# Pacing the input loads of a fused attention and token-mixing kernel by waiting on the landing of earlier loads

## The chip, the cores and the metric

The kernel runs on one core of one Trainium2 chip. The metric is the device time of one execution in microseconds (us). A run counts as slow when it is over 1.5% above the fastest run of the same kernel. Spans quoted from a profile are one or two us shorter than the times, as they run from the first to the last instruction.

## The reference

Chunked attention over 8 batches, 8 heads, 576 positions and head size 64, in chunks of 64 positions, then a token mixer over the 512 channels. Cut to what matters:

```python
scores = scale * np.matmul(q_c, k_c.transpose(0, 1, 2, 4, 3))   # chunks of 64 x 64
attn = softmax(scores)
x = np.matmul(attn, v_c)                       # -> [8, 576, 512]
wq, wk = x @ w_q, x @ w_k                      # 64 columns each
W_tok = scale * np.einsum('bsd,btd->bst', wq, wk)
mixed = np.einsum('bst,btd->bsd', W_tok, x)
out = np.maximum(mixed, 0.0) @ w_out           # [8, 576, 512], float32
```

The inputs q, k and v are 9.4 MB each in float32; the output is 9.4 MB.

## The kernel before

GpSimd (POOL) issues all loads; they cast float32 to float16 on the way. A batch takes twelve of them in this order: four large pieces of q and k, four half as large, two small and two large pieces of v. They go to fixed buffers (one q and k buffer per batch, four v buffers for eight batches). The load of the output weights follows batch 1. The code is cut; `...` stands for what is left out.

```python
TR = ((0, 6), (6, NT))                 # NT = 9: q and k in a part of 6 and one of 3
VP = ((0, 12, 0), (12, NP, 1))         # NP = 36: v in a part of 12 and one of 24

def load_qk(b, part):
    a, e = TR[part]
    for src, dst in ((q, qn), (k, kn)):
        for u in range(2):
            nc.gpsimd.dma_start(dst[b][CH*u : CH*u+CH, a:e, :], ...)

def load_v(b):
    for a, e, w in VP:
        for u in range(2):
            h = CH * (u ^ w)
            nc.gpsimd.dma_start(vt[b % VB][h : h+CH, a:e, D*u : D*u+D], ...)

def load(b):
    load_qk(b, 0)
    load_qk(b, 1)
    load_v(b)
    if b == 1:
        nc.gpsimd.dma_start(wout[:], ...)

load(0)
# ... identity, four small loads of the query and key weights ...
for b in range(1, VB):                 # VB = 4
    load(b)
# load(b + 4) is put after the attention of batch b in the plan of units
# ... a written plan orders transposes (T), scores (S), attention (A) and the
#     matmuls of the mixer (X Q K G M O) of several batches on TensorE;
#     all stores are held back until the v buffer of batch 7 is being filled ...
```

A piece of q or k from the larger part carries the weight 1 in what follows; a piece of v from the larger part carries 1.33. I call the loads of one batch q1 q2 k1 k2 q3 q4 k3 k4 v1 v2 v3 v4.

The softmax here doesn't subtract the row's maximum and nothing guards it: scores larger than these inputs give would overflow.

## Time and profile before

| | before |
|---|---|
| time, median of 4 runs | 127.09 us (126.0 to 128.57) |
| span of the profiled run (fast) | 124.5 us |
| TensorE busy | 100.3 us, 81% |
| first q piece of batches 3 to 7 lands at | 41.7, 52.7, 62.9, 73.6, 83.7 us: 10.5 us per batch |
| last load lands at | 93.1 us |
| k transposes of batches 3 to 7 start at | 48.0, 59.3, 71.8, 82.9, 94.7 us: 11.7 us per batch |

The landings come from the trace's semaphore events; each load has sixteen (one per DMA engine, by the section on semaphores that the prediction cites), and the sixteenth is its landing. The k transposes show the pace that TensorE keeps when nothing starves it. The loads run 1.2 us per batch faster than that. The lines of the profile are in the prediction below; here is the view of GpSimd's waits (engine, line, what it waited for; us in total, times, longest):

```profile
POOL kn L107 <- DMA vt<-in_v_dram: 7.6, 11, 1.5
POOL vt L118 <- issue: 2.4, 5, 0.8
POOL kn L107 <- DMA wout<-in_moe_w_out_dram: 1.5, 1, 1.5
```

GpSimd waits little, and mostly when eight loads are outstanding, the most that its eight semaphores in rotation allow.

### The profile page before, as it was taken

The page shows a single profiled execution, that of the slowest core. Times are in us where ns is not written, and L with a number is a line of the kernel's source. Part 1 is how long each engine was busy: PE and PEld are TensorE (multiplying, and loading weights), DVE is VectorE, ACT ScalarE, POOL GpSimd, SP SyncE. Part 2 cuts the span into 40 slices and gives each one's busy share as a digit, 9 for nine tenths or more (in the row PEclk, how much of TensorE's full clock was granted, in tenths as well). Part 3 has the DMA queues.
Part 4 walks back from the last instruction along what each step waited for, and adds up shares of the span by engine and source line. Part 5 has one row for each costly group of instructions (what it writes and reads, how often), then busy time and mean ns, then how long its engine had stood idle before and what let it go on. Part 6 is the DMA issues. An engine that isn't in the chain of part 4 may idle for free.

```text
span 124.5 us, 4600 instructions
## 1 busy us (share of the span) xinstructions
PE 100.3 (81%) x1959; PEld 61.8 (50%) x1959; DVE 75.4 (61%) x138; ACT 80.9 (65%) x138; POOL 72.0 (58%) x107
## 2 busy tenths in 40 slices
PE   6803280799639999999997899999999995999970
PEld 2203150587426565645764457656674674544420
DVE  5529079746873689759938695798599557400000
ACT  7992320514636486695687598686878793688960
POOL 6999799954769779589669958966400000000000
PEclk9997555559996899999999999999999999999998
DMA  1999999999999999999999999999999989964494
GB/s 10 171 183 156 155 167 169 153 152 196 194 156 165 189 175 143 186 189 150 159 182 167 152 188 185 145 189 189 154 223 342 383 325 380 381 238 170 169 348 160
DMA packets 63129, 24.55 MB, mean 197 GB/s; under 512 B 39556, under 2 KB 58500, under 8 KB 63108
## 3 DMA queue, kind: packets, MB, share of 16 engines
q0 software_dynamic: 57936, 14.82, 129.0%
q1 hardware_dynamic: 5172, 9.44, 20.3%
q8 instruction: 15, 0.25, 0.8%
q14 instruction: 6, 0.05, 0.1%
HBM read 29.62 MB, written 9.44 MB: 314 GB/s over the span
## 4 chain that ended last, share of the span: by engine, by line
PE 47%; DMA 17%; POOL 13%; DVE 11%; ACT 5%; issue 5%; DVEq 0%; ACTq 0%; POOLq 0%
PE banks L341 20%; DMA vt<-in_v_dram 9%; DMA kn<-in_k_dram 8%; PE banks L208 6%; DVE kT L181 6%; PE banks L273 5%; PE banks L234 5%; POOL kn L107 5%; PE banks L258 4%; POOL qn L107 4%; POOL vt L118 4%; DVE xn L244 3%; PE banks L306 3%; PE banks L320 2%; DVE rec L243 1%
## 5 line engine op out<-in xcount | busy, mean ns | idle before, releaser
L341 PE MATMUL banks<-wout,rmx 128*128 128x512 f16 x144 | 36.5, 386 | 0.0
L118 POOL DMA_DIRECT2D vt<-in_v_dram x32 | 27.3, 859 | 6.2 <-issue 2.4
L216 ACT ACTIVATE est<-banks 128x768 f16<-128x768 f32 x24 | 18.6, 810 | 17.8 <-PE banks L208 17.7
L244 DVE TENSOR_TENSOR xn<-banks,rec 128x640 f16<-128x640 f32 x32 | 26.4, 824 | 1.1
L107 POOL DMA_DIRECT2D kn<-in_k_dram x32 | 20.9, 668 | 9.1 <-DMA vt<-in_v_dram 7.6
L208 PE MATMUL banks<-qT,kT 32*64 32x64 f16 x1152 | 13.8, 218 | 11.5 <-DVE qT L181 5.3
L181 DVE STREAM_TRANSPOSE kT<-kn 128x768 f32<-128x768 f32 (+1 forms) x16 | 19.3, 1205 | 4.9 <-DMA kn<-in_k_dram 4.9
L328 ACT ACTIVATE rmx<-banks 128x576 f16<-128x576 f32 x32 | 19.6, 660 | 3.8 <-PE banks L320 3.7
L107 POOL DMA_DIRECT2D qn<-in_q_dram x32 | 21.1, 681 | 0.9 <-POOLq L417 0.8
L208 PEld LDWEIGHTS <-kT 32*64 32x64 f16 x1152 | 11.9, 112 | 14.8 <-DVE kT L181 10.0
L341 PEld LDWEIGHTS <-rmx 128*128 128x128 f16 x144 | 12.3, 98 | 13.6 <-issue 2.2
L234 PE MATMUL banks<-vt,est 128*64 128x130 f16 x288 | 15.8, 241 | 3.4 <-DMA vt<-in_v_dram 1.8
L243 DVE RECIPROCAL rec<-banks 128x10 f32<-128x10 f32 x32 | 6.8, 213 | 17.3 <-PE banks L234 14.2
L263 DVE COPY xt<-banks 128x576 f32<-128x576 f32 x16 | 11.9, 754 | 7.3 <-PE banks L258 5.2
L234 PEld LDWEIGHTS <-est 128*64 128x64 f16 x288 | 11.5, 119 | 8.0 <-issue 3.7
L258 PE MATMUL banks<-identw,xn 128*128 128x128 f32 x80 | 13.3, 307 | 2.2 <-DVE xn L244 1.6
L258 PEld LDWEIGHTS banks<-identw,xn 128*128 128x128 f32 x80 | 10.4, 156 | 5.6 <-DVE xn L244 2.6
L181 DVE STREAM_TRANSPOSE qT<-qn 128x768 f32<-128x768 f32 (+1 forms) x16 | 12.1, 757 | 0.5 <-DMA qn<-in_q_dram 0.5
L359 ACT COPY qn<-banks 128x512 f32<-128x512 f32 x16 | 9.5, 595 | 4.0 <-DVE xt L263 2.4
L359 ACT COPY kn<-banks 128x512 f32<-128x512 f32 (+1 forms) x15 | 9.2, 626 | 3.4 <-PE banks L341 3.1
L273 PE MATMUL banks<-xt,wqk 128*128 128x288 f16 x64 | 9.5, 289 | 0.0
L282 ACT CAST wT<-banks 128x576 f16<-128x576 f32 x8 | 5.1, 640 | 5.2 <-PE banks L273 5.2
(36 smaller groups left out, 88.4 us busy)
## 6 DMA issues: line engine op xcount, KB each, us to landing
out_dram<-qn SPq DMA_DIRECT2D x16, 256.0 KB, 3.9
out_dram<-kn SPq DMA_DIRECT2D x14, 256.0 KB, 2.9
qn<-in_q_dram POOLq DMA_DIRECT2D x16, 192.0 KB, 6.0
kn<-in_k_dram POOLq DMA_DIRECT2D x16, 192.0 KB, 6.8
vt<-in_v_dram POOLq DMA_DIRECT2D x16, 192.0 KB, 6.0
qn<-in_q_dram POOLq DMA_DIRECT2D x16, 96.0 KB, 6.9
kn<-in_k_dram POOLq DMA_DIRECT2D x16, 96.0 KB, 5.9
vt<-in_v_dram POOLq DMA_DIRECT2D x16, 96.0 KB, 5.2
```

The source lines that it names most:

```text
L107: nc.gpsimd.dma_start(dst[b][CH * u : CH * u + CH, a:e, :], src[b] .rearrange("h s d -> (h s) d") .rearrange("(u t p r) d -> u p t (r d)", ...
L118: nc.gpsimd.dma_start(vt[b % VB][h : h + CH, a:e, D * u : D * u + D], v[b] .rearrange("h s d -> (h s) d") .rearrange("(u g p) d -> u p g d ...
L181: nc.vector.transpose(out=o, in_=src[b].bitcast(F32)[:, a:e, :].rearrange("p t (r d) -> p t r d", d=32),)
L208: nc.tensor.matmul(a[h : h + CH, i, o : o + CH], lhsT=k_of(*x), rhs=q_of(*x), start=(e == 0), stop=(e == 1),)
L216: nc.scalar.activation(est[b % 2][s + n].rearrange("p i t c -> p i (t c)"), a[:, :, 0 : 2 * TS * CH], AF.Exp, scale=scale_attn,)
L234: nc.tensor.matmul(af[CH * (c % 2) : CH * (c % 2) + CH, o : o + W], lhsT=lhsT, rhs=rhs, start=True, stop=True,)
L244: nc.vector.tensor_tensor(out=xn[b % 2] .rearrange("p j (a u b d) -> p j a u b d", a=2, u=2, b=2)[:, :, h // 2, :, h % 2, :], in0=xv[:, :, ...
L258: nc.tensor.transpose(tx[:, j * P : j * P + P], xn[b % 2].bitcast(F32)[:, j, n * P : n * P + P], identw[:],)
L273: nc.tensor.matmul(a[:, h, 0:HS], lhsT=wqk[:, i, :], rhs=xt[b % 2][i // 2] .bitcast(F16) .rearrange("p (s e) -> p s e", e=2)[:, h * HS : h ...
L328: nc.scalar.activation(rmx[(b // 2) % 2].rearrange("p (h i) n -> p i h n", h=2)[:, i, :, o : o + HS], a[:, :, 0:HS], AF.Relu, scale=scale_moe,
L341: nc.tensor.matmul(a[:, x, :], lhsT=rmx[pr % 2][:, i, tl * P : tl * P + P], rhs=wout[:, 2 * (i % 2) + i // 2, :], start=(i == 0), stop=(i ...
L359: nc.scalar.copy(os_, a[:, 0:w, :])
```

## The change

Its intent is to keep only about four pieces outstanding, so that the pieces land in order and soon after their issue. Each load is given an estimate of its transfer time as a weight; it waits for the latest earlier load before which the weights still in flight sum to over 3.6. The diff is cut; `<semaphore wait>` stands for the object that describes the dependency.

```diff
+    AHEAD = 3.6
+    queue = []
+
+    def fetch(dst, src, us):
+        ins = nc.gpsimd.dma_start(dst, src).ins
+        ahead = 0.0
+        for name, u in reversed(queue):
+            if ahead + u > AHEAD:
+                tc.add_manual_dep(ins, name, <semaphore wait>, reason="pace")
+                break
+            ahead += u
+        queue.append((ins.name, us))
+
     def load_qk(b, part):
...
-                nc.gpsimd.dma_start(
+                fetch(
                     dst[b][CH * u : CH * u + CH, a:e, :],
...
+                    (e - a) / 6,
                 )
     def load_v(b):
...
-                nc.gpsimd.dma_start(
+                fetch(
...
+                    (e - a) / 18,
                 )
...
-            nc.gpsimd.dma_start(wout[:], ...)
+            fetch(wout[:], ..., 2.6)
```

More of the change, by code (lines that the diff above doesn't have):

```diff
@@ L101 @@
     of = out.rearrange("b s m -> (b s) m")
+    queue = []
[4 more added lines that the diff above has]
+            if ahead + u > AHEAD:
+                tc.add_manual_dep(
+                    ins,
+                    name,
+                    mybir.DependencyInfo(mybir.DependencyClass.Sync, mybir.DependencyReason.DATA),
+                    reason="pace",
+                )
+                break
+            ahead += u
+        queue.append((ins.name, us))
     def load_qk(b, part):
@@ L146, in load @@
         if b == 1:
-            nc.gpsimd.dma_start(wout[:], moe_w_out.rearrange("(i p) m -> p i m", p=P))
+            fetch(wout[:], moe_w_out.rearrange("(i p) m -> p i m", p=P), 2.6)
     nc.vector.memset(zero[:], 0.0)
```

## The prediction

> **What bounds the kernel now.** I read the page first: its busy shares, its forty slices and the list of DMA queues.
>
> ```profile
> span 124.5 us, 4600 instructions
> PE 100.3 (81%) x1959; PEld 61.8 (50%) x1959; DVE 75.4 (61%) x138; ACT 80.9 (65%) x138; POOL 72.0 (58%) x107
> ...
> PE   6803280799639999999997899999999995999970
> ...
> PEclk9997555559996899999999999999999999999998
> DMA  1999999999999999999999999999999989964494
> ...
> q8 instruction: 15, 0.25, 0.8%
> ...
> HBM read 29.62 MB, written 9.44 MB: 314 GB/s over the span
> ```
>
> One slice is 3.1 us. TensorE (PE) is broken up in the first twelve slices and close to full in all that follow. The DMA engines are full from the second slice until the loads end near 93 us. So there are two regimes: to about 37 us TensorE waits for data, from there to the end it has work all the time. The table of windows says the same with sums:
>
> ```profile
> 0.00:12.00 12.00, 5.47 (x110) 2.63 (x110) 6.77 (x30) 8.92 (x13) 10.87 (x21) 0.95 1.25 129
> 12.00:24.00 12.00, 5.47 (x205) 3.91 (x189) 7.09 (x12) 3.27 (x5) 11.33 (x18) 0.50 1.78 161
> 24.00:37.00 13.00, 9.17 (x180) 6.87 (x180) 8.85 (x15) 5.76 (x11) 7.98 (x13) 0.85 1.72 174
> 37.00:55.00 18.00, 17.67 (x398) 11.10 (x394) 12.39 (x20) 12.37 (x21) 14.48 (x22) 0.91 1.84 174
> 55.00:75.00 20.00, 18.53 (x409) 11.35 (x403) 15.97 (x25) 14.66 (x27) 16.34 (x24) 1.00 1.86 167
> ```
>
> The columns are the window, its length, busy time of PE, PEld, DVE, ACT and POOL, the granted clock, the DMA share and GB/s. TensorE is busy 20.1 of the first 37 us, and 36.2 of the next 38.
>
> Next came the chain of waits, for what ends the idle time. These are three places of it, all before 37 us:
>
> ```profile
> 7.92 6.29 DMA vt<-in_v_dram
> 14.20 0.28 issue
> 14.49 0.66 POOL kn L107
> ...
> 24.60 10.43 DMA kn<-in_k_dram
> 35.05 1.53 DVE kT L181
> 36.63 0.98 PE banks L208 x96
> ```
>
> The piece of k for batch 2 is issued at 24.60 and lands at 35.03; the transpose starts 0.02 us later, and the scores of batch 2 (S02) at 36.63. TensorE idles 2.15 us before them. That is the last wait for a load which I find: in the list of waits the 4.9 us of the k transposes on loads all lie before 37 us, and between 37 and 95 us no compute engine waits for a load. **The load stream matters only as far as it moves that landing at 35.0 us.**
>
> The first two lines above also show a limit that exists already. GpSimd (POOL) issues at 14.49, 0.29 us after a v piece issued eight transfers earlier landed. In the trace's semaphore numbers the loads rotate over eight semaphores, and each waits for the one eight before it. So at most eight are outstanding now; the change makes that about four.
>
> **What the Trainium skill says.** "DMA: Bandwidth & Descriptors", section "Anatomy of one DMA", puts the fixed cost of a GpSimd DMA at about 2.0 us and says that semaphore waits sit on the issuing sequencer, not on the DMA engines. The trace: the first piece is issued at 1.25, its descriptors take 0.78, and it lands at 4.61, so 2.58 us after them. With a transfer near 1.05 us that leaves 1.5 us fixed plus the issue: roughly agreed. The same page, "Specifications", gives about 358 GB/s of HBM per core. Here 29.62 MB are read from about 2.7 to 92.5 us, 330 GB/s, 92% of it: agreed, the stream is near its ceiling. The section "Why a DMA increments its semaphore by 16 and not by 1" says that sixteen engines each add one and only the sixteenth means landed. The trace has sixteen events per load. For the first piece they span 0.43 us, for the k piece that lands at 35.02 they span 2.86 us (first 32.16, median 33.11). "TensorE: Matmul & The Clock Gate", Part 1, says that the clock is halved after an idle window. Here it was 0.50 in 12 to 24 us, and the clock records also have 0.5 from 38.1 to 41.5 us, just after the stall: agreed.
>
> **The change part by part.** It removes and moves no transfer, no byte and no arithmetic. It adds a wait to each load except the first few and the four small loads of the query and key weights.
>
> *How deep the queue stays.* The weights in the diff are 1 four times, 0.5 four times, 0.67 twice and 1.33 twice: 10 per batch, and 2.6 for the output weights. First issues of later batches stand at 46.27, 56.78, 67.45 and 77.93 in GpSimd's timeline, 10.55 us per batch or 1.055 us per unit of weight. Walking the rule over a batch, the weight in flight with the new piece is between 3.33 (second q piece, second v piece) and 4.67, against eight pieces or about 6.7 today.
>
> *Whether that keeps the engines fed.* The round trip of a paced piece of weight 1 is 0.29 (landing to issue, above) + 0.68 (mean of the q and k issues, page rows 668 and 681 ns) + 2.58 (descriptors ready to landed) = 3.55 us. A depth of 4 covers 4.2 us, so 0.7 us is spare; the tightest, 3.33, covers 3.51 us, so 0.04 us is missing, once per batch. After the output weights only the two q pieces remain ahead of the next k piece, so 3 units or 3.17 us: 0.39 us missing, once. Up to the landing at 35 us the sum is some 0.5 us lost.
>
> *Start.* The v pieces of batch 0 now wait for k landings at 7.21, 8.61 and 9.64. The fourth is issued at about 10.5 instead of 8.89; the identity (about 0.5 us) and four unpaced weight loads of 0.6 us follow it on GpSimd, so the first q piece of batch 1 goes out at about 14.4 instead of 12.70. With 0.7 + 2.2 to 2.6 us it lands near 17.5 instead of 16.56. But the following pieces then land one unit apart, near 20.65 instead of 20.27: 0.4 us lost.
>
> *Spread.* The engines that run ahead are now held back. When one engine falls behind, the others can be no more than about 0.7 us ahead of it before they run dry, so the spread of 2.86 us should shrink to about 1. If the common limit is HBM, the late engine gets what the others leave, and the landing moves from 35.0 towards its median of 33.1: 1.0 to 1.9 us gained. If each engine is its own limit, the others merely idle. Then each stall of one engine stalls all. Such stalls exist: the fifteen instruction packets take 0.8% of sixteen engines' span, 0.008 x 16 x 124.5 / 15 = 1.06 us each, and three start before 35 us. That would cost 1 to 2 us.
>
> *Sum at that landing.* +0.5 +0.4 and then between -1.9 and +2, weighing a gain somewhat higher because that landing's spread is so large: -0.3 us, give or take 1.5. Behind it everything moves along, as TensorE is saturated.
>
> **The rivals.**
> 1. *A clear gain.* The landing comes 2 us earlier, so the gap of 2.15 us closes, and the half-clock window from 38.1 to 41.5 us, which costs up to 1.7 us, goes with it. For it: the gap lies just before the window. Against it: it needs nearly all of the spread and no bubble. About 124 us.
> 2. *A starved stream.* The waits let the load rate fall by a tenth, so that batch 3 is late too. Its k piece lands at 44.52 and is transposed at 48.04, 3.5 us of margin; batch 4's lands at 55.35 for 59.25, 3.9 us. The margins speak against it; the thin spare depth speaks for it. 129 to 131 us.
> 3. *Hidden anyway.* Loads take 10.55 us per batch and TensorE about 12 us, so from 37 us on the waits cost nothing, and v pieces already wait for their buffer. The loads may even end 2 to 4 us later; the held stores start at 89.8 us and have a reserve behind them in a tail bound by TensorE. Within 1% of before.
>
> **How range and chances follow.** Rival 3 with a shift of -0.3 us is the centre. The three times before are 126.0, 127.83 and 128.57 and the profiled run took 126.24, so 127.5 is a fair level for before and I put the changed kernel at 127.2. The shift of 1.5 us either way and the spread of the runs of 1.3 us give 124.6 to 129.8. Two per cent are 2.6 us: a gain of that size needs rival 1 in full, a loss needs rival 2. A pacing with weights as fine as these looks swept for, which tips the tails towards faster: 0.20, 0.65 and 0.15.
>
> **What would show it.** In the changed trace: no more than about four load pieces outstanding; GpSimd idle before nearly every load with a load as the releaser; median time to landing of q and k pieces down from 6 to 7 us to about 4; spread of the sixteen increments near 1 us. The k piece for batch 2 landing at 33.5 to 36 us decides the sign. TensorE's slices after 37 us should be as full as before. The prediction is wrong if the landing stays and the time moves (then the clock or the stores did it), or if a transpose after 40 us waits for a load (then the stream was starved).

## The result

The changed kernel takes **144.07 us** (median of four runs, 142.15 to 147.01) against 127.09. The ratio of the fast runs is 1.127, with a 95% interval of 1.103 to 1.150. Here and below a ratio is the mean time of one kernel's fast runs over that of the other's of the same rounds, so not quite the ratio of the medians. The prediction of 127.2, at most 129.8, was wrong, and the change is slower beyond doubt.

The profile after is of a run in the slow state (144.74 us; two of the four runs were fast, 142.15 and 143.4). Its main readings, the wait of q2 and what it costs, were found again in a profile of a fast run with that wait alone, below; its exact times hold for this run only. The page of the changed kernel, its busy shares, slices (3.6 us each here) and the first DMA queue:

```profile
span 143.0 us, 4618 instructions
...
PE   6604342889549977967876899698679996999920
...
PEclk9995555556986999999996899999999999999997
DMA  2999999999999599969994999999999999999994
...
q0 software_dynamic: 57936, 14.82, 109.7%
```

TensorE is no longer full from 37 us on: its row has 5s, 6s and 7s up to the loads' end at 116 us. The DMA row has dents (5, 6, 4). The same packets took about the same time in sum (109.7% of 143.0 us against 129.0% of 124.5 us) but overlapped less. GpSimd's waits in the changed kernel, where all loads are now issued from one line:

```profile
POOL qn L107 <- DMA vt<-in_v_dram: 20.2, 6, 4.5
POOL vt L107 <- DMA kn<-in_k_dram: 5.2, 7, 1.1
POOL qn L107 <- DMA qn<-in_q_dram: 2.4, 2, 1.3
```

A q piece waits for a v piece, six times, 20.2 us in all. The timeline of GpSimd shows where it stands in a batch (start, length, what, idle time before and what ended it):

```profile
67.78 3.48 POOL L107 DMA_DIRECT2D vt<-in_v_dram  x4 [1.29 <-PE banks L340]
71.53 0.66 POOL L107 DMA_DIRECT2D qn<-in_q_dram  x1 [0.28 <-issue]
76.05 0.66 POOL L107 DMA_DIRECT2D qn<-in_q_dram  x1 [3.86 <-DMA vt<-in_v_dram]
76.70 1.32 POOL L107 DMA_DIRECT2D kn<-in_k_dram  x2
```

It is q2: the weights of q1, v4 and v3 make 3.67, just over the limit, so it waits for v3 with only 2.33 units left in flight. The chain that ended last runs through the same place:

```profile
69.36 6.17 DMA vt<-in_v_dram
75.52 0.02 issue
75.55 0.02 POOLq L107
75.56 0.49 issue
76.05 0.43 POOL qn L107
```

v3 is issued at 69.36 and lands at 75.52, and q2 leaves at 76.05. The first pieces of batches 3 to 7 land at 48.4, 63.1, 77.2, 92.1 and 105.0 us: **14.1 us per batch instead of 10.5**, slower than the 11.7 us at which TensorE works. The transposes now wait for loads in the middle of the kernel (timeline of the changed kernel on VectorE, called DVE, which does them; the first k transposes of batches 3, 4 and 6):

```profile
54.02 1.57 DVE L201 STREAM_TRANSPOSE kT<-kn 128x768 f32<-128x768 f32 x1 [0.18 <-DMA kn<-in_k_dram]
68.35 1.58 DVE L201 STREAM_TRANSPOSE kT<-kn 128x768 f32<-128x768 f32 x1 [0.37 <-DMA kn<-in_k_dram]
...
96.63 1.66 DVE L201 STREAM_TRANSPOSE kT<-kn 128x768 f32<-128x768 f32 x1 [0.67 <-DMA kn<-in_k_dram]
```

These waits are short, 0.2 to 0.7 us. TensorE itself waits longer, for v pieces: 6.7 us in four waits between 40 and 112 us, where the kernel before had no wait of TensorE for a load between 37 and 95 us. There is one in each of batches 3 to 6, and it ends when v4, the last load of the batch, lands (the whole view of TensorE's waits in the kernel before from 37 to 95 us, then of the changed kernel from 40 to 112 us its first line, and the line of its timeline for batch 4, whose v4 lands at 76.20):

```profile
PE banks L306 <- issue: 1.0, 2, 0.6
PE banks L258 <- DVE xn L244: 0.4, 1, 0.4
PE banks L208 <- DVE kT L181: 0.2, 1, 0.2
...
PE banks L254 <- DMA vt<-in_v_dram: 6.7, 4, 2.2
...
76.25 0.54 PE L254 MATMUL banks<-vt,est 128*64 128x130 f16 x6 [2.04 <-DMA vt<-in_v_dram]
```

The span grew by 18.5 us (by 15.9 and 17.1 in the two fast runs, which have no profile). The k transpose of batch 7 starts 16.0 us later (110.70 against 94.74). From the scores after it to the last ACT copy both kernels take the same, 24.3 and 24.4 us. The remaining 2.4 us are at the end: from the end of that copy the last stores take 5.65 us instead of 3.2. The held stores were released at 112.95 us, not at 89.84, and were still in arrears when TensorE finished.

### The profile page after: what moved, and what is told of

Its sections match the earlier page's. It is cut to its first block, busy times and chain, and to the rows that moved or that the text cites. A ratio compares the mean times of both kernels' runs of the same rounds, so it can differ in the third digit from the quotient of the medians.

```text
span 143.0 us, 4618 instructions
## 1 busy us (share of the span) xinstructions
PE 104.5 (73%) x1959; PEld 64.2 (45%) x1959; DVE 75.8 (53%) x138; ACT 81.6 (57%) x138; POOL 72.0 (50%) x107
## 3 DMA queue, kind: packets, MB, share of 16 engines
q0 software_dynamic: 57936, 14.82, 109.7%
## 4 chain that ended last, share of the span: by engine, by line
DMA 47%; PE 19%; POOL 16%; issue 8%; DVE 4%; ACT 2%; POOLq 0%; DVEq 0%; ACTq 0%
DMA vt<-in_v_dram 21%; DMA kn<-in_k_dram 18%; POOL vt L107 10%; PE banks L361 9%; DMA wout<-in_moe_w_out_dram 5%; DMA qn<-in_q_dram 3%; POOL qn L107 2%; PE banks L254 2%; PE banks L326 2%; DVE xn L264 2%; POOL kn L107 2%; PE banks L340 2%; POOL wraw L176 2%; PE banks L228 2%; PE banks L293 2%
## 5 line engine op out<-in xcount | busy, mean ns | idle before, releaser
L361 PE MATMUL banks<-wout,rmx 128*128 128x512 f16 x144 | 37.5, 394 | 0.1
L107 POOL DMA_DIRECT2D qn<-in_q_dram x32 | 20.7, 655 | 24.8 <-DMA vt<-in_v_dram 20.2
L254 PE MATMUL banks<-vt,est 128*64 128x130 f16 x288 | 17.0, 246 | 10.7 <-DMA vt<-in_v_dram 9.6
L228 PE MATMUL banks<-qT,kT 32*64 32x64 f16 x1152 | 14.0, 219 | 14.5 <-DVE qT L201 5.9
L228 PEld LDWEIGHTS <-kT 32*64 32x64 f16 x1152 | 12.1, 114 | 18.1 <-DVE kT L201 12.7
L254 PEld LDWEIGHTS <-est 128*64 128x64 f16 x288 | 12.1, 121 | 16.4 <-issue 8.3
L361 PEld LDWEIGHTS <-rmx 128*128 128x128 f16 x144 | 12.6, 100 | 13.9 <-issue 2.6
L278 PEld LDWEIGHTS banks<-identw,xn 128*128 128x128 f32 x80 | 10.8, 161 | 6.3 <-DVE xn L264 3.1
L293 PE MATMUL banks<-xt,wqk 128*128 128x288 f16 x64 | 10.4, 308 | 0.0
L340 PE MATMUL banks<-wT,g 64*128 64x288 f16 x32 | 7.5, 287 | 2.6 <-DVE xn L264 1.8
```

The source lines that it names most:

```text
L107: ins = nc.gpsimd.dma_start(dst, src).ins
L228: nc.tensor.matmul(a[h : h + CH, i, o : o + CH], lhsT=k_of(*x), rhs=q_of(*x), start=(e == 0), stop=(e == 1),)
L254: nc.tensor.matmul(af[CH * (c % 2) : CH * (c % 2) + CH, o : o + W], lhsT=lhsT, rhs=rhs, start=True, stop=True,)
L278: nc.tensor.transpose(tx[:, j * P : j * P + P], xn[b % 2].bitcast(F32)[:, j, n * P : n * P + P], identw[:],)
L293: nc.tensor.matmul(a[:, h, 0:HS], lhsT=wqk[:, i, :], rhs=xt[b % 2][i // 2] .bitcast(F16) .rearrange("p (s e) -> p s e", e=2)[:, h * HS : h ...
L361: nc.tensor.matmul(a[:, x, :], lhsT=rmx[pr % 2][:, i, tl * P : tl * P + P], rhs=wout[:, 2 * (i % 2) + i // 2, :], start=(i == 0), stop=(i ...
```

## The experiments

I had three theories. **S**: every load is waited for until the slowest of the sixteen engines has it, and single late engines use the small depth up. **D**: the depth is too small for the round trip as such. **W**: the added waits cost GpSimd time, whatever the depth.

Summary of the timed runs (four runs of each, of the kernel before seven beside each group; load period is from the profiled run, first q piece of batch 3 to that of batch 7, divided by four; the medians include slow runs, the ratios don't; the profiles of the changed kernel and of the last row are of slow runs, all others of fast ones):

| kernel | median us | ratio, 95% interval | load period us | last landing us |
|---|---|---|---|---|
| before | 127.0 / 127.11 | 1 | 10.5 | 93.1 |
| changed, limit 3.6 | 144.07 | 1.127, 1.103 to 1.150 | 14.1 | 116.4 |
| limit 3.7 | 136.43 | 1.079, 1.071 to 1.087 | 12.4 | 109.0 |
| limit 5.0 | 127.93 | 1.009, 1.000 to 1.019 | 11.5 | 99.6 |
| limit 6.3 | 127.09 | 1.004, 0.992 to 1.017 | 10.7 | 95.5 |
| only q2 paced | 137.47 | 1.084, 1.074 to 1.093 | 12.7 | 109.4 |
| batches 0 to 2 paced | 132.49 | 1.044, 1.035 to 1.053 | 10.6 | 99.9 |
| batches 3 to 7 paced | 137.43 | 1.071, 1.058 to 1.083 | 14.2 | 112.6 |

### The dose: limits of 3.7, 5.0 and 6.3

```diff
-    AHEAD = 3.6
+    AHEAD = 3.7      # e1;  5.0 in e2;  6.3 in e3
```

> The changed kernel with the limit at 3.7 instead of 3.6, so that the second q piece of a batch waits for the load four back (3.67 units ahead) instead of three back (2.33), likewise one v piece in two places. Theory S (a late engine eats the depth: every load waits for the slowest of sixteen engines, and the depth of 2.33 to 3.5 units is used up when one engine is 1.5 us late): one more v piece of about 1.4 us at the worst place, so about 1 to 1.5 us less per batch, 132 to 138 us. Theory W (the waits themselves cost GpSimd time): as many waits as before, no change, 142 to 146 us.

> Limit 5.0, depth 4.0 to 5.0 units ahead. Theory S: the spare depth of about 1 to 1.7 us covers a stall of 1.5 us nearly everywhere, batch period of the loads about 11 us, 127 to 130 us. Theory W: nearly as many waits, 138 us or more.

> Limit 6.3, depth 5.0 to 6.0 units ahead, hardly under the eight pieces that the rotation of semaphores allows anyway. Theory S: within 1% of the kernel before, 126 to 128.5 us. Theory W: still above 135 us where waits are added.

All three came out as the theories of depth (S and D) have it, and W falls: with nearly as many waits in the code, 5.0 gives back all but 0.9% and 6.3 all but 0.4%, which is not clear of zero. Going from 3.6 to 3.7 alone gives back 7.6 us. It lets one more piece of v stay in flight when q2 is issued (3.67 units instead of 2.33), and one more piece at v2 and v4. The step from 12.4 to 11.5 us per batch is worth more than a proportional share, 136.4 to 127.9 us. Two things change there, and these runs don't separate them: 11.5 is just under TensorE's 11.7 us per batch, and the start is no longer late. The second large k piece of batch 2 lands at 39.0 us with a limit of 3.7 and at 35.0 with 5.0, as in the kernel before; what a late start alone costs is measured under "Early or late".

### One wait alone

All pace waits are taken out but that of q2.

```diff
-            if ahead + u > AHEAD:
+            if keep and ahead + u > AHEAD:   # keep: larger part of q, second half
```

> The changed kernel with all pace waits taken out but the one of the second q piece of each batch, which waits for the third v piece of the batch before with 2.33 units ahead. If the loss sits at single shallow places (theory S, as the per-position table of the loads suggests), this one wait costs 1.1 to 1.8 us per batch, the loads take 11.6 to 12.4 us per batch, and the kernel 128 to 134 us. If the loss is spread over all waits (theory W), under 128 us.

It took 137.47 us, more than the upper end of 134, and 12.7 us per batch, more than 12.4. So **one wait per batch makes 10.4 of the 17 us**. The profile, of a fast run, shows it as nearly the only pause of GpSimd (26.6 us of idle time in seven waits, and 3.4 us in three others):

```profile
65.28 0.68 POOL L107 DMA_DIRECT2D qn<-in_q_dram  x1
70.37 0.66 POOL L107 DMA_DIRECT2D qn<-in_q_dram  x1 [4.42 <-DMA vt<-in_v_dram]
71.02 1.33 POOL L107 DMA_DIRECT2D kn<-in_k_dram  x2
```

### Loads alone, with and without a TensorE program

To tell S from D, I took all compute out. The loads and their waits stay in order, the stores write zeros (the result is wrong). In two of the four kernels 1900 small matmuls on a tile of zeros run beside the loads, needing none of them. The point of those: TensorE's instructions come in by the same DMA engines, as packets of 16 KB on the queue that the profile calls "instruction". In the kernel before, fifteen of them took 0.88 to 1.54 us each; the two runs without a TensorE program have none on that queue.

```diff
-    for u in PLAN.split(): ...
+    for b in range(VB, B):
+        load(b)
+    for n in range(1900):                  # e7 and e8 only
+        nc.tensor.matmul(banks[:, n % 8, 0:64], lhsT=zero[:, 0:P], rhs=zero[:, 0:64], ...)
```

> Loads alone, result wrong on purpose: no compute, all loads of the kernel before in its order without pacing, then stores of zeros. Without a TensorE program there are no instruction packets during the loads. Both theories: about 10 to 10.4 us per batch, all sixteen engines within about 1 us of each other.

> Loads alone with pacing at 3.6, result wrong on purpose, no TensorE program and so no instruction packets. Theory S (stalls of one engine are what the shallow queue cannot absorb): 10.5 to 11.5 us per batch. Theory D (the depth of 2.33 to 3.5 units is too small for the round trip by itself, with no stall needed): 13.5 to 14.5 us per batch as in the whole kernel.

> Loads alone without pacing, result wrong on purpose, beside 1900 small TensorE matmuls that use no loaded data, so that its instruction packets come in during the loads. Theory S and D: the deep queue absorbs the stalls, 10.2 to 10.8 us per batch, spread of the increments of a load up to 2 us.

> Loads alone with pacing at 3.6 beside the same 1900 matmuls, result wrong on purpose. Theory S: each instruction packet (1.0 to 1.5 us on one engine) costs the whole stream about 1 us or more, so 1 to 2.5 us per batch above the paced run without matmuls, depending on how many packets fall in a batch. Theory D: the same period as the paced run without matmuls.

| loads alone | period us | last landing us |
|---|---|---|
| free | 10.5 | 93.0 |
| paced | 12.6 | 109.1 |
| free, with matmuls | 10.8 | 95.8 |
| paced, with matmuls | 13.5 | 116.5 |

From batch to batch the free loads vary between 9.7 and 11.3 us, so that 10.5 against 10.8 is not a clear difference, while 2.1 us is. The paced loads without any instruction packet fall between what S (10.5 to 11.5) and D (13.5 to 14.5) expected: **both are at work**. Of the 3.6 us per batch that the changed kernel loses, 2.1 are there without compute and without packets. Beside the matmuls the paced stream loses another 0.9 on average, just under the 1 to 2.5 that S expected. Within that run the effect can be seen coming and going: batch to batch it takes 14.5, 14.4, 13.1 and 12.0 us, against 13.4, 12.3, 12.7 and 12.1 without matmuls; the packets end at 71.6 us, during the second of these, and the matmuls at 75.1. The last 0.6 of the 3.6 us is not explained. One part may be the waits of v pieces for a buffer that TensorE still reads, which loads alone don't have: 2.0 us in two waits in the changed kernel, one of them in the timeline above ("PE banks").

One expectation failed: the free loads without packets were to have all sixteen engines within about 1 us of each other, and their median spread is 1.80 us. So the spread of the free stream is not the packets' doing. GpSimd's waits in the paced loads without matmuls show the same place as before:

```profile
POOL qn L107 <- DMA vt<-in_v_dram: 14.7, 7, 3.4
POOL vt L107 <- DMA kn<-in_k_dram: 4.5, 10, 1.0
POOL kn L107 <- DMA wout<-in_moe_w_out_dram: 3.5, 1, 3.5
```

How one packet acts is seen in the sixteen events of v3 in the changed kernel, batch 4 (us, from the semaphore events). An instruction packet of 1.53 us began at 72.12:

```
73.09 73.10 73.13 73.17 73.25 73.29 73.31 73.40 73.50 73.51 73.58 73.64 73.75 73.85 73.90   75.52
```

Fifteen engines are done by 73.90. The sixteenth is 1.6 us late, and q2 waits for it. The late sixteenth is also there in v3 of batches 1, 2 and 3, and each time a packet began 2.4 to 3.5 us before that landing. In v3 of batches 5, 6 and 7 no packet began in that stretch, and the sixteenth is at most 0.12 us behind the fifteenth. The same holds over all loads of the changed kernel that land between 20 us and the end of TensorE's work: the sixteenth event is 0.78 us behind the fifteenth on average for the 24 that land 1 to 4 us after the start of a packet, and 0.23 us for the other 59. The records don't name the engine, so that it is the packet's engine which is late is inferred from the time. What the runs above measure is the cost of a TensorE program beside the loads, packets and matmuls together; that it is the packets which act rests on these events.

### One load at a time

> Loads alone, each waiting for the landing of the one before it, no compute, result wrong on purpose: it measures the round trip of each size of piece by itself. From the first piece of the kernel before: about 3.3 us from issue to landing for a piece of weight 1, and 0.29 us from landing to the next issue. If the round trip is longer in the middle of a kernel than at its start, or the issue later after a landing, the prediction's 3.55 us was too short: 3.8 to 4.2 us per unit piece.

Loads alone, with the limit so low that each waits for the one before (`AHEAD = 0.1`). The table of DMA issues has the round trip of each size, in its last column, from issue to landing:

```profile
qn<-in_q_dram POOLq DMA_DIRECT2D x16, 192.0 KB, 3.5
kn<-in_k_dram POOLq DMA_DIRECT2D x16, 192.0 KB, 3.5
vt<-in_v_dram POOLq DMA_DIRECT2D x16, 192.0 KB, 4.1
qn<-in_q_dram POOLq DMA_DIRECT2D x16, 96.0 KB, 2.6
```

A piece of weight 1 takes 3.5 us by itself, hardly more than the 3.36 us of the first load before. From a landing to the next issue it was 0.28 us nearly everywhere here; in the changed kernel q2 was issued 0.28 us after the landing in two of four batches and 0.53 us after it in the other two, where a separate semaphore instruction came first. From one large q or k landing to the next it is 3.7 to 3.8 us, just under the expected 3.8 to 4.2, so the prediction's 3.55 was somewhat short, but this is not where the loss comes from.

### Early or late

The waits of only batches 0 to 2, or only batches 3 to 7, were kept.

```diff
-            if ahead + u > AHEAD:
+            if ahead + u > AHEAD and b < 3:      # e10;  b >= 3 in e11
```

> Pacing of batches 0 to 2 only. The k piece of batch 2 lands at about 39.5 us as in the changed kernel (35.0 before), and from there the loads run at 10.5 us per batch, under the 12 us or so that TensorE needs: the 4 to 4.5 us stay, 130 to 132.5 us. If the late start were made up for later, 127 to 129 us.

> Pacing of batches 3 to 7 only. The start is as before (k piece of batch 2 at 35 us), then 14 us per batch: last landing at about 110 us instead of 93, TensorE waits from batch 4 or 5 on, 136 to 140 us. If the margins of 3.5 us and more which the kernel before had were enough, 126 to 128.5 us.

Both as expected by the first sentence of each. Early pacing makes the second large k piece of batch 2 (k2) land at 39.2 us instead of 35.0 and the kernel 4.4% slower; the delay is not made up for. Late pacing starts as before (35.6 us) and then runs at 14.2 us per batch, 7.1% slower. The two add to 11.5%, near the 12.7% of both together.

### A miss: the output weights later

With the landing of that k load called decisive, moving the load of the output weights behind q1 to k2 of batch 2 should pay in the kernel before.

```diff
     def load(b):
         load_qk(b, 0)
+        if b == 2:
+            nc.gpsimd.dma_start(wout[:], ...)
         load_qk(b, 1)
         load_v(b)
-        if b == 1:
-            nc.gpsimd.dma_start(wout[:], ...)
```

> The kernel before, no pacing, with the 2.6-unit load of the output weights moved behind the first four q and k pieces of batch 2. If the landing of the k piece of batch 2 at 35.0 us is what ends the first regime, it comes 2 us earlier and the kernel takes 124.5 to 126 us. If something else holds TensorE there (the wait of DVE and ACT on batch 1), no change, 126 to 128.5 us.

The k load landed at 31.7 us, 3.3 us earlier, but the ratio is 0.996 (0.986 to 1.005). A gain of over 1.4% is ruled out, one of half a per cent is not. So that landing matters when it comes later, as the early pacing shows, but bringing it forward frees little. What takes its place was not found. No version here clearly beats the kernel before.

## Why the prediction was wrong, point by point

**Its first reading held.** The two regimes, the last wait for a load before 37 us and the limit of eight outstanding loads are all as described. What followed from "the load stream matters only as far as it moves that landing" did not hold, as it took the load rate for given.

**The step that failed first: "the tightest, 3.33, covers 3.51 us, so 0.04 us is missing, once per batch".** The step was right in kind: the time from a landing to the landing that it sets free must be covered by what is in flight. Its terms were wrong in size. From v3's mean landing to q2's mean landing (mean over the sixteen events, v3 of batches 3 to 6 and q2 of the batch after; us):

| term | predicted | paced loads alone | changed kernel |
|---|---|---|---|
| v3's sixteenth event after its mean | none | 0.62 | 1.29 |
| landing to issue of q2 | 0.29 | 0.41 | 0.41 |
| issue to landing of q2 | 3.26 | 3.32 | 3.31 |
| **sum** | **3.55** | **4.35** | **5.01** |
| covered by v4, q1 and q2 in the free stream | 3.51 | 3.25 | 3.19 |
| **missing** | **0.04** | **1.10** | **1.82** |

The cover in the last column is from the kernel before, that in the middle one from the free loads alone. The fast run with the wait of q2 alone has 1.42, 0.41 and 3.28 us in the first three rows. The largest error is a term left out: a wait waits for the slowest of sixteen engines, while the stream moves at their mean. The prediction knew the spread and used it only as a possible gain. Without this lateness 0.48 of the 1.10 and 0.53 of the 1.82 us would still be missing: at this place the late engines are the larger part of the loss, and the small depth as such is the rest. The next error is the cover: it put 1.055 us on each unit of weight, but v4 and the two q pieces took 1.48 to 1.50, 0.87 to 0.91 and 0.82 to 0.86 us. The round trip itself was nearly right.

**Second, "once per batch" for the tightest place and 0.7 us spare elsewhere.** Comparing the mean step from one load to the next over batches 4 to 7, the other eleven places of the changed kernel still lose 1.6 us per batch: k2 0.39, v1 0.33, v3 0.27, v2 0.21, the rest under 0.2 each. With the wait of q2 alone they lose 0.6 us, so that part of this follows from q2. A spread of over 1 us exceeds a spare of 0.7.

**Third, the spread as a gain.** The median spread of the sixteen events did fall, from 1.80 to 1.24 us. But the landings came later, and the busy share of the DMA engines has dents: the late engine did not make use of what the others left. Of its two cases the prediction gave more weight to the wrong one. The other, "each stall of one engine stalls all", is what the sixteen events of v3 show.

**Fourth, the start and the output weights.** Among the k landings that hold back the v pieces of batch 0 the prediction lists 9.64 us, which is q4's; k3's is 10.23. It also left out that q3 waits for q1: it was issued at 5.05 us instead of 3.95, and the fourth v piece at 11.30, not 10.5. The first q piece of batch 1 was to land near 17.5 us and came at 18.9; k2 of batch 1 was to land near 20.65 and came at 22.55 (20.27 before). From the last v piece of batch 1 to k2 of batch 2, past the output weights, 1.7 us were lost (8.81 us against 7.08), not 0.39. The landing given as -0.3 us, give or take 1.5, moved by +4.5 us.

**Fifth, the margins.** Rival 2 named the mechanism, a starved stream, and was dismissed for margins of 3.5 us and more. Margins cover a delay that happens once. Here the load period rose past TensorE's 11.7 us, so that the delay grew with each batch, on top of a start that was 4.5 us late. The rival also sized the loss of rate at a tenth; the period grew by a third, so the rate fell by a quarter.

**Sixth, the stores and the clock.** The reserve behind the held stores was not enough: 2.4 us at the end. TensorE's busy time rose by 4.2 us (104.5 against 100.3): its clock records have 0.5 in 11.1 to 35.0, 41.9 to 45.3 and 76.0 to 79.4 us, against 10.8 to 27.9 and 38.1 to 41.5 before. In the 3.4 us before the last two windows TensorE was busy for only 1.0 and 1.6 us. That fits the starving and the clock section that the prediction cites; no run here tests it apart.

Of the signs listed at its end, fewer loads outstanding (three to six from batch 2 on, the new one counted, against six to eight) and q and k landings at 4.0 to 5.1 us after issue came true. They only show that the pacing works as meant. GpSimd idle "before nearly every load" did not: its view of waits has a load as the releaser 22 times, for 101 loads, which fits a few tight places and not waits everywhere. The sign for "starved", a transpose after 40 us that waits for a load, came too.

## What to carry to other kernels

Before limiting how many transfers are outstanding, sum up the whole loop at its tightest place: lateness of the slowest engine, landing to issue, issue to landing, against the measured time of exactly those pieces that remain in flight, and leave at least the observed spread as spare (here 1.24 us at a limit of 3.6). A short latency per load is no gain where the stream is the bound and the data is not needed sooner. Compare the rate that results with the rate of the consumer, and not the delay with the margin.

## What the Trainium skill lacked or had wrong

- "DMA: Bandwidth & Descriptors", section "Anatomy of one DMA": its fit of 2.0 us plus bytes over 436 GB/s gives 2.9 us, an estimate, for a piece that reads 393 KB (64 partitions, cast on the way). One load at a time took 3.5 us for q and k and 4.1 us for v, whose rows in HBM are a quarter as long. For such pieces the fit is 0.6 to 1.2 us too short.
- The same section calls descriptor generation small, while the page's section "Latency and other measured facts" has about 1 us to the first byte on account of it. Here it occupies GpSimd for about 0.62 to 0.98 us per load, so it is a visible term of the loop, and the second is the nearer.
- "Runtime: NRT & Kernel Launch", section "Instruction fetch mechanics", has instructions fetched by DMA in blocks of 16 KiB and calls the cost mostly hidden. No page says how long such a packet takes or what it does to a load that lands with it. Here one took 0.88 to 1.54 us, and paced loads alone went from 12.6 to 13.5 us per batch beside a TensorE program.
- No page says how many transfers a paced stream needs. Here, with pieces of about 1 us: a limit of 3.6 cost 12.7%, 3.7 cost 7.9%, 5.0 cost 0.9%, and 6.3 nothing clear.
